# Attention and sixteen experts on one core: the last two units' means rows move to ScalarE's DMA queue, and the last steps of the hand-written order are moved

## The chip, the cores and the metric

The kernel runs on one core of a Trainium2 chip. The metric is the device time of one execution in microseconds (us), the median over the runs. The engines are TensorE (PE), VectorE (DVE), ScalarE (ACT), GpSimd (POOL) and SyncE (SP), which only issues DMAs and loads values.

## The reference

Attention over 8 batches, 8 heads, 576 positions and 64 dimensions per head, in two parts that are added; then a mixture of 16 experts over the 4608 tokens of 512 dimensions:

```python
q_d, k_d, v_d = means of four neighbouring positions      # 144 of each
out_d = softmax(q_d k_d^T / 8) v_d, repeated four times
mask = |i - j| < 4
out_local = softmax(q k^T / 8 where mask) v
x = out_d repeated + out_local                            # 4608 x 512
g = argmax(x @ w_group);  e = argmax(x @ w_expert[g])     # 4 groups of 4
out[token] = p_group * p_expert * (relu(x @ w1[g, e]) @ w2[g, e])
```

## The kernel before

The attention is cut into 16 units; unit u is a pair of batches times a pair of heads, four units to a pair of batches. For every unit the local part is computed as scores in a band, and out_local and the repeated out_d come out of one matmul: the values of the windows (tile vw, `windows(u)`) have rows for the window's positions and, between them, rows for the means' attention (`load_down`). So a unit goes through these steps, each a method of `Attention`:

- `load_k`, `load_q`, `load_v`, `load_windows`: loads, all on SyncE's queue.
- `pool_q`, `pool_k`, `pool_v`: sums over four positions (tiles qd, kd, vd), for late units on GpSimd (L215 to L217), except pool_q of 15.
- `s_down` (L314): scores of the means from kd and qd; `s_down_max`, `s_down_exp` (ScalarE, L348, tile Pd), `soft_down` (L354 on GpSimd, tile sg, then two instructions on VectorE).
- `turn_pd`, `turn_pd_out`, `out_down` (L401), `out_down_out`, `turn_down` (L412), `turn_down_out` (VectorE, tile odn).
- `down_store` (L429, L430): the means' attention goes to DRAM (odd) over SyncE's queue. `load_down` (L434): it comes back into the rows of the windows tile (vw<-odd), over the queue that the order names: S is SyncE's, A is ScalarE's.
- `turn_e`, `turn_e_out`: the band's probabilities, turned (tile pt). `x_bank` (L441, three banks of matmuls b_x<-vw,pt), `x_bank_out` into the tile x (L165 on ScalarE, L167 on VectorE), `store_x` (L451) to the table xd in DRAM, `turn_x`, `logits` (L486, L489).

Tiles that are kept from unit to unit are chosen by `of`: x has three tiles, x_124 in a pool that stays and x_125, x_126 in the pool inp, which is closed by the step `change` and whose room the first expert's tiles take over. Units below 14 take them in turn, units 14 and 15 take the first, so unit 12 is in x_124, unit 13 in x_125, and units 14 and 15 both in x_124.

After each pair of batches the router (`Router`) chooses an expert per token, and its steps `weight` (a small store xd<-cw, L661), `places`, `places_out`, `count`, `lists` (tile m, L671), `lists_places`, `lists_add` and `lists_out` build the experts' token lists. From the first three pairs `pick_early` takes one expert; `early_list` builds its list of 256 tokens of units 0 to 11 (gi), `early_expert` (L1361) reads its number on SyncE, `change` opens the expert's pools, and `gather` (L851) fetches the tokens (xg) by an indirect DMA of GpSimd. Its weights come in four quarters: `weights_in` c (two DMAs raww on SyncE, L831) and `weights_split` c into a high and a low part (ScalarE L838, then GpSimd or VectorE L839). `turn_in` (L867) turns the tokens, `hidden` f (L880) is the first matmul of eighth f, `project` f (L926) the second. When the last pair's lists are there, `gather_late` fetches the expert's remaining tokens, `ranks` sorts the experts by load (VectorE, L787 to L1100; tile roh at L789), and `turn_late` turns the remaining tokens. Then `main` runs the other experts, one after the other, on TensorE.

What sets the order: everything up to `project 7` is issued in the order of the string `ORDER` (L1213 to L1324) inside a manual schedule. An entry is a step, its unit, and sometimes the engine or queue. Each engine works through its instructions in that order and waits at each for what it needs.

Of the kernel before, what the change touches and what calls it, by code (L numbers as in the profile page):

```python
# [54 lines left out]
class Attention:  # L55
# [1254 lines left out]
load_windows 15; s_local_exp 15 1; turn_x_out 13 2 A; out_down 15; lists_places 2; turn_x 13 0; soft_down 15 P; turn_x 13 1; lists 2 P  # L1310
out_down_out 15 A; turn_down 15; turn_x_out 13 1 A; turn_down_out 15; turn_x_out 13 0 A; load_down 14 S; down_store 15 S; early_expert
lists_add 2; turn_e 14 2; logits 13; turn_e 14 1; early_list 1; turn_e_out 14 2 A; change; gather; turn_e 14 0; lists_out 2
turn_e_out 14 1 A; turn_e_out 14 0 A; x_bank 14 2; x_bank 14 0; x_bank 14 1; x_bank_out 14 0 A; x_bank_out 14 1 A; turn_x 14 0
soft_local_sum 15 D; soft_local 15; x_bank_out 14 2 D; turn_e 15 0; store_x 14 A; turn_e_out 15 0 D; turn_x_out 14 0 D; turn_x 14 2
turn_x 14 1; turn_x_out 14 1 D; turn_x_out 14 2 A; weights_in 0; turn_e 15 1; turn_in 0; turn_e_out 15 1 D; weights_split 0 w1 P
load_down 15 S; logits 14; turn_in 1; weights_split 0 w2 P; weights_in 1; turn_e 15 2; turn_e_out 15 2 D; x_bank 15 0; turn_in 2
x_bank_out 15 0 A; x_bank 15 1; x_bank_out 15 1 A; x_bank 15 2; x_bank_out 15 2 D; turn_in 3; weights_in 2; turn_x 15 1; turn_x 15 2
turn_x_out 15 2 D; store_x 15 S; turn_x 15 0; weights_split 1 w1 P; turn_x_out 15 1 D; turn_x_out 15 0 A; hidden 0; weights_split 1 w2 P
weights_in 3; logits 15; scores_out 3; hidden 1; scores_turn 3; project 0; scores_turn_out 3; choose 3; choose_exp 3; choose_first 3
weight 3; hidden 2; project 1; places 3; places_out 3; project 2; weights_split 2 w1 P; lists_places 3; lists 3 P; count 3  # L1320
weights_split 2 w2 P; hidden 3; hidden 4; hidden 5; lists_add 3; early_list 0; gather_late; project 3; ranks; weights_split 3 w1 P
# [107 lines left out]
```

## Time and profile before

| | |
|---|---|
| median of 3 runs | 754.81 us |
| the runs | 747.65, 755.3, 754.81 us |
| the profiled execution | 745.63 us |
| its span in the profile | 743.7 us |
| TensorE busy in the span | 696.0 us (94%) |
| VectorE, ScalarE, GpSimd busy | 461.6, 388.5, 252.9 us |
| mean granted TensorE clock | 0.981 of full |

The profiled execution is one execution by itself; the rows below are from it. Times in the rows are microseconds from the start of the span. A row of a timeline has its start, its duration, the engine, the line, the tiles written and read, how many instructions it joins (x3), and in brackets how long the engine had been idle before it and what released it. A row with "SPq" or "ACTq" is the issue of a DMA, not its transfer.

### The profile page before, as it was taken

Reading aid. Unit: us, or ns where it says so; the run is one execution under the profiler, and the core shown is the slowest. Engines: PE = TensorE matmul, PEld = TensorE weight load, DVE = VectorE, ACT = ScalarE, POOL = GpSimd, SP = SyncE. Lnnn points to the kernel's source line nnn. Section 1 sums busy time; section 2 is a strip of 40 time slices with the busy share of each in tenths; the row PEclk is TensorE's granted clock in tenths of the full one; section 3 lists DMA queues with packets and bytes.
Section 4 is the critical chain, followed back from the end, with each engine's and each line's share of the span. In section 5 each row is a group of like instructions: output and inputs, shape, how many; then the busy total and the mean of one; then the engine's idle time right before and its main releaser. Section 6 shows DMA issues by size and latency. Waiting matters only on the chain. (4 is left out here: it accounts for less than half of the span.)

```text
span 743.7 us, 17951 instructions
## 1 busy us (share of the span) xinstructions
PE 696.0 (94%) x7134; PEld 627.0 (84%) x7135; DVE 461.6 (62%) x821; ACT 388.5 (52%) x830; POOL 252.9 (34%) x301
## 2 busy tenths in 40 slices
PE   7788987898987988999999999999999999999997
PEld 4566765676665867998999999999999999999996
DVE  6777877888885766654545454464655565565641
ACT  6766746666674425643434444454554554555531
POOL 7956654576533633003211221302213213212211
PEclk9889999999999999999999999999999999999999
DMA  9979898889879456845455555646555665665600
GB/s 295 258 182 253 253 279 253 201 221 255 220 189 264 121 163 185 274 152 185 150 169 171 163 171 174 206 142 218 172 186 186 206 201 191 221 191 198 222 31 26
DMA packets 109912, 144.94 MB, mean 195 GB/s; under 512 B 22737, under 2 KB 78545, under 8 KB 109825
## 3 DMA queue, kind: packets, MB, share of 16 engines
q1 hardware_dynamic: 85216, 113.25, 51.9%
q0 software_dynamic: 7088, 21.66, 8.5%
q10 hardware_dynamic: 17520, 8.85, 4.7%
q8 instruction: 57, 0.93, 0.5%
q14 instruction: 31, 0.25, 0.1%
HBM read 122.43 MB, written 22.29 MB: 195 GB/s over the span
## 5 line engine op out<-in xcount | busy, mean ns | idle before, releaser
L880 PE MATMUL ph<-xh,w1h 128*128 128x256 f32 (+13 forms) x512 | 161.1, 316 | 0.0
L851 POOL DMA_INDIRECT xg<-xd,gi x47 | 49.1, 1044 | 324.3 <-ACT yo L954 289.9
L880 PE MATMUL ph<-xl,w1h 128*128 128x256 f32 (+13 forms) x512 | 156.0, 306 | 0.0
L880 PE MATMUL ph<-xh,w1l 128*128 128x256 f32 (+13 forms) x512 | 156.0, 307 | 0.0
L839 DVE TENSOR_TENSOR w2l<-raww,w2h 128x1024 fp32r<-128x1024 f32 x61 | 74.6, 1224 | 75.2 <-ACT w2h L838 61.6
L928 PE MATMUL y<-hl,w2h 128*128 128x416 f32 (+11 forms) x384 | 115.3, 311 | 0.0
L928 PE MATMUL y<-hh,w2l 128*128 128x416 f32 (+11 forms) x384 | 114.3, 308 | 0.0
L838 ACT ACTIVATE w2h<-raww 128x1024 fp32r<-128x1024 f32 x64 | 67.5, 1057 | 74.3 <-PE y L928 56.0
L880 PEld LDWEIGHTS ph<-xh,w1h 128*128 128x128 f32 x512 | 96.2, 188 | 1.4 <-issue 0.2
L880 PEld LDWEIGHTS ph<-xl,w1h 128*128 128x128 f32 x512 | 96.3, 188 | 0.9
L839 DVE TENSOR_TENSOR w1l<-raww,w1h 128x1024 fp32r<-128x1024 f32 x60 | 73.4, 1224 | 37.6 <-ACT w1h L838 31.6
L880 PEld LDWEIGHTS ph<-xh,w1l 128*128 128x128 f32 x512 | 96.1, 188 | 0.3
L885 DVE SCALAR_TENSOR_TENSOR hl<-ph,hh 128x256 fp32r<-128x256 f32 (+13 forms) x128 | 60.3, 477 | 54.8 <-ACT hh L884 52.2
L884 ACT ACTIVATE hh<-ph 128x256 fp32r<-128x256 f32 (+13 forms) x128 | 53.9, 422 | 71.6 <-PE ph L880 66.3
L928 PE MATMUL y<-hh,w2h 128*128 128x416 f32 (+11 forms) x384 | 87.7, 312 | 0.0
L838 ACT ACTIVATE w1h<-raww 128x1024 fp32r<-128x1024 f32 x64 | 67.5, 1056 | 30.5 <-PE ph L880 24.2
L928 PEld LDWEIGHTS y<-hh,w2l 128*128 128x128 f32 x384 | 72.3, 188 | 0.1
L928 PEld LDWEIGHTS y<-hl,w2h 128*128 128x128 f32 x384 | 72.2, 188 | 0.1
L955 POOL DMA_INDIRECT out_dram<-yo,oi x47 | 47.8, 1017 | 66.5 <-ACT yo L954 53.0
L928 PEld LDWEIGHTS y<-hh,w2h 128*128 128x128 f32 x384 | 62.9, 188 | 0.1
L860 ACT ACTIVATE xh<-xt 128x256 fp32r<-128x256 f32 (+14 forms) x68 | 27.0, 420 | 38.3 <-PE xt L867 35.7
L441 PE MATMUL b_x<-vw,pt 126*32 126x128 f32 x1152 | 40.4, 284 | 4.0 <-DMA vw<-odd 2.0
(227 smaller groups left out, 1286.6 us busy)
## 6 DMA issues: line engine op xcount, KB each, us to landing
raww<-in_moe_w_dram SPq DMA_DIRECT2D x128, 512.0 KB
vw<-in_vw_dram SPq DMA_DIRECT2D x32, 378.0 KB
kt<-in_k_dram SPq DMA_DIRECT2D x16, 576.0 KB
qT<-in_q_dram SPq DMA_DIRECT2D x16, 576.0 KB
xd<-x ACTq DMA_DIRECT2D x15, 576.0 KB
vs<-in_vm_dram SPq DMA_DIRECT2D x16, 448.0 KB
vw<-odd SPq DMA_DIRECT2D x16, 144.0 KB
vs<-in_vm_dram SPq DMA_DIRECT2D x16, 128.0 KB
```

Source lines behind the costliest of these rows:

```text
L441: self.nc.tensor.matmul(pt[32 * j : 32 * j + 32, t], self.of("pt", u)[:ROWS, 32 * lin : 32 * lin + 32], self.windows(u)[:ROWS, :, lin], st ...
L838: self.nc.scalar.activation(hi, raw, AF.Copy)
L839: eng.tensor_tensor(out=lo, in0=raw, in1=hi.bitcast(F32), op=ALU.subtract)
L851: self.nc.gpsimd.indirect_dma_start(out=xg[:w], out_offset=None, in_=self.xd[0:rows], in_offset=bass.IndirectOffsetOnAxis(ap=st["gi"][:w, ...
L860: self.nc.scalar.activation(hi, x, AF.Copy)
L880: nc.tensor.matmul(ph, a[:, k, cs], st[b][:, k], start=(n == 0), stop=(n == 11))
L884: nc.scalar.activation(hh, ph, AF.Relu)
L885: nc.vector.scalar_tensor_tensor(out=hl, in0=ph, scalar=0.0, in1=hh.bitcast(F32), op0=ALU.max, op1=ALU.subtract)
L928: nc.tensor.matmul(y, a[:, f % 2, cs], b, start=(f == 0 and n == 0), stop=(f == 7 and n == 2))
L955: i = nc.gpsimd.indirect_dma_start(out=self.out, out_offset=bass.IndirectOffsetOnAxis(ap=oi, axis=0), in_=yo[:m], in_offset=None, bounds_c ...
```

## The change

Three things are changed, and nothing in the steps themselves.

- `of` gives the tile x differently for units 12 to 15: unit 12 goes to x_125, units 13 and 14 to x_124, and unit 15 to the first 1152 columns of the windows tile of unit 14 (vw_100), which x_bank 14 has read by then.
- `load_down` of units 14 and 15 stands on ScalarE's queue: the first behind out_down_out 15, the second between two copies of x_bank 14.
- The last 22 lines of `ORDER` are written anew (21 now). On SyncE load_v 15, load_windows 14 and weight 2 stand ahead of load_down 13. On GpSimd soft_down 14 stands ahead of pool_k 15. Of the third pair's router places_out, count, lists_places, lists, pick_early, lists_add and lists_out stand further up, and with them early_list and gather. turn_pd_out 15 2 goes from VectorE to ScalarE. Of the early expert's weights the splits of quarters 2 and 3 stand further up and w2 of quarter 3 goes from VectorE to GpSimd; hidden 6 stands ahead of the four steps turn_late, which were two and two around it.

```diff
@@ class Attention
     def of(self, n, u):
 
         t = self.kept[n]
+        if n == "x" and u > 11:
+            return (t[1], t[0], t[0], self.vw[0][:, 0, 0 : 2 * G].rearrange("p (g a) d -> p g (a d)", a=2))[u - 12]
         return t[u % len(t) if u < LATE_UNITS else 0]
...
@@ ORDER
-turn_pd 14 0; turn_pd 14 2; turn_x_out 12 1 A; turn_pd_out 14 0 A; turn_pd_out 14 2 A; pool_k 15 P; pick_early; turn_pd 14 1; s_down 15
-load_v 15; turn_pd_out 14 1 A; turn_x 12 2; store_x 12 A; turn_x_out 12 2 A; load_windows 14; soft_down 14 P; out_down 14; x_bank 13 1
+soft_down 14 P; soft_local_sum 14 D; turn_x_out 12 0 A; turn_pd 14 0; turn_pd 14 2; turn_x_out 12 1 A; turn_pd_out 14 0 A
+turn_pd_out 14 2 A; pool_k 15 P; turn_pd 14 1; s_down 15; turn_pd_out 14 1 A; turn_x 12 2; store_x 12 A; turn_x_out 12 2 A; out_down 14
...
-project 4; project 5; turn_late 0; turn_late 1; hidden 6; turn_late 2; turn_late 3; hidden 7; weights_split 3 w2 D; project 6; rank_lists
-project 7
+project 4; project 5; hidden 6; turn_late 0; turn_late 1; turn_late 2; turn_late 3; hidden 7; project 6; rank_lists; project 7
```

Behind `of` the kernel after is two lines longer, so L434 is L436 there and so on.

GpSimd around pool_k 15 (kd_3594 from kt_91), before; sg_118 is soft_down 14, vd_112 is pool_v 15, m the third pair's lists:

```order
L217 TENSOR_TENSOR vd_111<-vd_111,vs_115 112x384
L215 TENSOR_TENSOR kd_3594<-kt_91 128x288
L216 TENSOR_TENSOR kd_3594<-kd_3594,kt_91 128x288
L217 TENSOR_TENSOR kd_3594<-kd_3594,kt_91 128x288
L354 TENSOR_SCALAR sg_118<-sg_118 128x5
L215 TENSOR_TENSOR vd_112<-vs_113 112x384
L216 TENSOR_TENSOR vd_112<-vd_112,vs_113 112x384
L217 TENSOR_TENSOR vd_112<-vd_112,vs_113 112x384
L354 TENSOR_SCALAR sg_119<-sg_119 128x5
L671 TENSOR_TENSOR m_3792<-oh,chl 128x9x64
```

The same place after, where pool_k 15 is kd_3626:

```order
L219 TENSOR_TENSOR vd_111<-vd_111,vs_115 112x384
L356 TENSOR_SCALAR sg_118<-sg_118 128x5
L217 TENSOR_TENSOR kd_3626<-kt_91 128x288
L218 TENSOR_TENSOR kd_3626<-kd_3626,kt_91 128x288
L219 TENSOR_TENSOR kd_3626<-kd_3626,kt_91 128x288
L217 TENSOR_TENSOR vd_112<-vs_113 112x384
L218 TENSOR_TENSOR vd_112<-vd_112,vs_113 112x384
L219 TENSOR_TENSOR vd_112<-vd_112,vs_113 112x384
L673 TENSOR_TENSOR m_3732<-oh,chl 128x9x64
L356 TENSOR_SCALAR sg_119<-sg_119 128x5
```

pool_k 15 stood ahead of soft_down 14 and now stands behind it; lists 2 has moved ahead of soft_down 15 (sg_119).

SyncE from load_windows 15 (vw_101) on, before; vw_100 is the windows tile of unit 14, odd the means' attention in DRAM, raww the early expert's weights:

```order
L200 DMA vw_101<-in_vw_dram 42x2x1152 x2
L434 DMA vw_100<-odd_89 8x72x64
L429 DMA odd_90<-odn_131 128x2x128
L430 DMA odd_90<-odn_131 32x128
L1361 TENSOR_LOAD eri_168
L1361 ISA x2
L831 ISA
L831 DMA raww_3944<-in_moe_w_dram 128x4x256
L831 ISA
L831 DMA raww_3946<-in_moe_w_dram 128x2x512
L434 DMA vw_101<-odd_90 8x72x64
L831 ISA
```

And after:

```order
L202 DMA vw_101<-in_vw_dram 42x2x1152 x2
L431 DMA odd_90<-odn_131 128x2x128
L432 DMA odd_90<-odn_131 32x128
L1362 TENSOR_LOAD eri_168
L1362 ISA x2
L833 ISA
L833 DMA raww_3945<-in_moe_w_dram 128x4x256
L833 ISA
L833 DMA raww_3947<-in_moe_w_dram 128x2x512
L833 ISA
L833 DMA raww_3980<-in_moe_w_dram 128x4x256
L833 ISA
```

Both load_down are gone from SyncE; the second pair of weights now follows the first directly.

ScalarE around the copies of x_bank 14 (x_124 from b_x_14), before:

```order
L165 ACTIVATE xT<-b_xt_13_3781 128x384
L165 ACTIVATE pt_122<-b_e_14_3827 126x384
L687 ACTIVATE tab<-tab_3816 128x128
L165 ACTIVATE pt_122<-b_e_14_3835 126x384
L165 ACTIVATE pt_122<-b_e_14_3870 126x384
L165 ACTIVATE x_124<-b_x_14_3890 128x384
L165 ACTIVATE x_124<-b_x_14_3903 128x384
L451 DMA xd<-x_124 128x9x128
L165 ACTIVATE xT<-b_xt_14_3934 128x3x128
```

And after:

```order
L167 ACTIVATE od_129<-b_od_3790 128x288
L436 DMA vw_100<-odd_89 8x72x64
L167 ACTIVATE xT<-b_xt_13_3803 128x384
L167 ACTIVATE xT<-b_xt_13_3799 128x384
L167 ACTIVATE pt_122<-b_e_14_3858 126x384
L167 ACTIVATE pt_122<-b_e_14_3866 126x384
L167 ACTIVATE pt_122<-b_e_14_3871 126x384
L167 ACTIVATE x_124<-b_x_14_3890 128x384
L436 DMA vw_101<-odd_90 8x72x64
L167 ACTIVATE x_124<-b_x_14_3903 128x384
L453 DMA xd<-x_124 128x9x128
L167 ACTIVATE xT<-b_xt_14_3935 128x3x128
```

load_down 14 (vw_100<-odd_89) stands behind out_down_out 15 (od_129), load_down 15 (vw_101<-odd_90) between the two copies of x_bank 14, one row and a copy ahead of store_x 14.

## Rows read from the trace of the kernel before

**Rows 1.** busy us by window, PE PEld DVE ACT POOL; granted clock; DMA share; GB/s

```profile
230.00:240.00 10.00, 7.29 (x118) 4.98 (x115) 3.85 (x9) 4.56 (x9) 3.44 (x2) 1.00 0.88 257
...
260.00:270.00 10.00, 6.61 (x39) 4.99 (x38) 8.56 (x19) 2.50 (x7) 3.17 (x2) 1.00 0.41 132
...
280.00:290.00 10.00, 8.06 (x37) 6.17 (x36) 4.71 (x8) 3.92 (x9) 2.60 (x2) 0.83 0.69 206
...
400.00:500.00 100.00, 100.00 (x676) 99.59 (x675) 52.58 (x73) 48.11 (x77) 18.15 (x18) 1.00 0.53 170
```

**Rows 2.** TensorE's timeline, 213 to 242 us: start, duration, line, tiles, [idle before <-releaser]

```profile
213.01 1.15 PE L314 MATMUL b_d<-kd,qd 64*128 64x144 f32 x20
...
228.12 1.94 PE L441 MATMUL b_x<-vw,pt 126*32 126x128 f32 x60 [2.03 <-DMA vw<-odd]
...
236.25 0.86 PE L441 MATMUL b_x<-vw,pt 126*32 126x128 f32 x24
...
240.29 0.44 PE L867 MATMUL xt<-idf,xg 128*128 128x128 f32 x2 [1.35 <-ACT x L165]
...
241.66 0.39 PE L880 MATMUL ph<-xh,w1h 128*128 128x256 f32 x1
```

**Rows 3.** ScalarE's timeline, 231 to 240 us (ACTq: its DMA issues)

```profile
231.49 0.37 ACTq L451 DMA_DIRECT2D xd<-x  x1
...
239.74 0.87 ACT L165 ACTIVATE x<-b_x 128x384 f32<-128x384 f32 x2 [1.77 <-DMA xd<-x]
```

**Rows 4.** GpSimd's timeline, 200 to 230 us

```profile
204.50 0.94 POOL L217 TENSOR_TENSOR kd<-kd,kt 128x288 f32<-128x288 f32 x1
211.80 0.20 POOL L354 TENSOR_SCALAR sg<-sg 128x5 f32<-128x5 f32 x1 [6.36 <-ACT Pd L348]
...
227.28 1.29 POOL L851 DMA_INDIRECT xg<-xd,gi  x1 [5.92 <-DMA odd<-odn]
```

**Rows 5.** SyncE's DMA issues, 226 to 242 us

```profile
226.28 0.98 SPq L831 DMA_DIRECT2D raww<-in_moe_w_dram  x2
228.44 0.77 SPq L434 DMA_DIRECT2D vw<-odd  x1
229.43 9.92 SPq L831 DMA_DIRECT2D raww<-in_moe_w_dram  x3
```

**Rows 6.** DMA by queue (packets, MB, share), 228 to 231 us: q1 SyncE's, q0 GpSimd's

```profile
q1 hardware_dynamic: 715, 0.96, 91.2%
```

**Rows 7.** DMA by queue, 231 to 233.5 us

```profile
q0 software_dynamic: 114, 0.35, 51.9%
q1 hardware_dynamic: 734, 0.33, 50.3%
```

**Rows 8.** DMA by queue, 233.5 to 236 us: q10 is ScalarE's

```profile
q1 hardware_dynamic: 552, 0.71, 95.0%
...
q10 hardware_dynamic: 2, 0.00, 0.1%
```

**Rows 9.** DMA by queue, 236 to 239 us

```profile
q10 hardware_dynamic: 1161, 0.59, 75.6%
```

**Rows 10.** TensorE's timeline, 262 to 270 us

```profile
263.17 0.44 PE L867 MATMUL xt<-idf,xg 128*128 128x128 f32 x2 [1.35 <-DMA xg<-xd,gi]
...
268.54 0.50 PE L926 MATMUL y<-w2h,hh 128*128 128x512 f32 x1 [1.48 <-ACT w2h L838]
...
269.80 0.50 PE L926 MATMUL y<-w2l,hh 128*128 128x512 f32 x1 [0.53 <-DVE w2l L839]
```

**Rows 11.** VectorE's timeline, 260 to 264 us

```profile
260.71 2.77 DVE L789 TENSOR_TENSOR roh<-rank,eidx 128x256 f32<-128x256 f32 x1
```

**Rows 12.** TensorE's timeline, 284 to 290 us

```profile
284.34 0.44 PE L904 MATMUL ht<-idf,hr 128*128 128x128 f32 x2 [1.15 <-ACT hr L899]
...
286.17 0.63 PE L926 MATMUL y<-w2h,hrl 128*128 128x512 f32 x1
...
289.22 0.39 PE L926 MATMUL y<-w2h,hrl 128*128 128x512 f32 x1
```

More of the change, by code (lines that the diff above doesn't have):

```diff
@@ L1302 @@
 x_bank 12 1; s_down 14; down_store 13 S; pool_q 15 D; load_windows 13; s_local_exp 15 0; lists_out 1; x_bank_out 12 1 A; choose_first 2
-x_bank 12 0; choose_exp 2; x_bank 12 2; s_down_max 14; x_bank_out 12 0 A; places 2; turn_x 12 0; load_down 13 S; turn_x 12 1
-soft_local_sum 14 D; x_bank_out 12 2 A; s_down_exp 14 0; pool_v 14; s_down_exp 14 2; s_down_exp 14 1; count 2; turn_x_out 12 0 A
-turn_pd 14 0; turn_pd 14 2; turn_x_out 12 1 A; turn_pd_out 14 0 A; turn_pd_out 14 2 A; pool_k 15 P; pick_early; turn_pd 14 1; s_down 15
@@ L1306 @@
-load_v 15; turn_pd_out 14 1 A; turn_x 12 2; store_x 12 A; turn_x_out 12 2 A; load_windows 14; soft_down 14 P; out_down 14; x_bank 13 1
-s_down_max 15; weight 2; s_down_exp 15 2; out_down_out 14 A; turn_down 14; x_bank 13 2; s_down_exp 15 0; s_down_exp 15 1; x_bank_out 13 1 A
-pool_v 15; x_bank 13 0; turn_pd 15 0; x_bank_out 13 2 A; turn_down_out 14; soft_local 14; x_bank_out 13 0 A; turn_pd_out 15 0 A
-places_out 2; store_x 13 A; turn_pd 15 1; down_store 14 S; turn_x 13 2; turn_pd 15 2; turn_pd_out 15 1 A; logits 12; turn_pd_out 15 2 D
@@ L1310 @@
[L1310 to L1321, printed above, removed]
@@ L1322 @@
-project 4; project 5; turn_late 0; turn_late 1; hidden 6; turn_late 2; turn_late 3; hidden 7; weights_split 3 w2 D; project 6; rank_lists
-project 7
+x_bank 12 0; choose_exp 2; x_bank 12 2; s_down_max 14; x_bank_out 12 0 A; places 2; load_v 15; load_windows 14; weight 2; turn_x 12 0
+load_down 13 S; turn_x 12 1; places_out 2; count 2; x_bank_out 12 2 A; s_down_exp 14 0; pool_v 14; s_down_exp 14 2; s_down_exp 14 1
+soft_down 14 P; soft_local_sum 14 D; turn_x_out 12 0 A; turn_pd 14 0; turn_pd 14 2; turn_x_out 12 1 A; turn_pd_out 14 0 A
@@ new lines @@
+turn_pd_out 14 2 A; pool_k 15 P; turn_pd 14 1; s_down 15; turn_pd_out 14 1 A; turn_x 12 2; store_x 12 A; turn_x_out 12 2 A; out_down 14
+x_bank 13 1; s_down_max 15; s_down_exp 15 2; out_down_out 14 A; turn_down 14; x_bank 13 2; s_down_exp 15 0; s_down_exp 15 1
+x_bank_out 13 1 A; pool_v 15; x_bank 13 0; turn_pd 15 0; x_bank_out 13 2 A; lists_places 2; turn_down_out 14; lists 2 P; soft_local 14
+pick_early; soft_down 15 P; x_bank_out 13 0 A; turn_pd_out 15 0 A; store_x 13 A; turn_pd 15 1; down_store 14 S; turn_x 13 2; turn_pd 15 2
@@ new lines @@
+turn_pd_out 15 1 A; turn_pd_out 15 2 A; logits 12; lists_add 2; load_windows 15; s_local_exp 15 1; turn_x_out 13 2 A; lists_out 2
+out_down 15; turn_x 13 0; turn_x 13 1; out_down_out 15 A; load_down 14 A; early_list 1; turn_down 15; turn_x_out 13 1 A; turn_down_out 15
+turn_x_out 13 0 A; down_store 15 S; early_expert; change; gather; turn_e 14 2; logits 13; turn_e 14 1; turn_e_out 14 2 A; turn_e 14 0
+turn_e_out 14 1 A; turn_e_out 14 0 A; x_bank 14 2; x_bank 14 0; x_bank 14 1; x_bank_out 14 0 A; load_down 15 A; x_bank_out 14 1 A
@@ new lines @@
+turn_x 14 0; soft_local_sum 15 D; soft_local 15; x_bank_out 14 2 D; turn_e 15 0; store_x 14 A; turn_e_out 15 0 D; turn_x_out 14 0 D
+turn_x 14 2; turn_x 14 1; turn_x_out 14 1 D; turn_x_out 14 2 A; weights_in 0; turn_e 15 1; turn_e 15 2; turn_in 0; turn_e_out 15 1 D
+weights_split 0 w1 P; logits 14; turn_in 1; weights_split 0 w2 P; weights_in 1; turn_e_out 15 2 D; x_bank 15 0; turn_in 2; x_bank_out 15 0 A
+x_bank 15 1; x_bank_out 15 1 A; x_bank 15 2; x_bank_out 15 2 D; turn_in 3; weights_in 2; turn_x 15 1; turn_x 15 2; turn_x_out 15 2 D
@@ new lines @@
+store_x 15 S; turn_x 15 0; weights_split 1 w1 P; turn_x_out 15 1 D; turn_x_out 15 0 A; hidden 0; weights_split 1 w2 P; weights_in 3
+logits 15; scores_out 3; hidden 1; scores_turn 3; project 0; scores_turn_out 3; weights_split 2 w1 P; choose 3; choose_exp 3
+weights_split 2 w2 P; choose_first 3; weight 3; hidden 2; project 1; places 3; places_out 3; project 2; lists_places 3; lists 3 P; count 3
+weights_split 3 w1 P; hidden 3; hidden 4; hidden 5; lists_add 3; early_list 0; gather_late; project 3; ranks; weights_split 3 w2 P
```

## The prediction

> **What bounds the kernel now.** I read the busy time by window first [rows 1]. From 400 to 500 us TensorE is busy for 100.00 of 100 us: the sixteen experts follow each other without a gap, so nothing the change does can shorten that part. What it can move is the moment at which TensorE becomes gapless. Before that moment stand 230 to 240 us with 7.29 us busy of 10, 260 to 270 us with 6.61, and 280 to 290 us with 8.06 at a granted clock of 0.83. Every microsecond by which TensorE's work up to about 290 us shifts goes straight into the end time, and nothing else does.
>
> Then I read TensorE's own timeline there for the waits [rows 2]. s_down of unit 15 starts at 213.01 with no wait. x_bank of unit 14 starts at 228.12, after 2.03 us of waiting for its means rows (vw<-odd, load_down 14). x_bank of unit 15 starts at 236.25 with none. At 240.29 TensorE has lost 1.35 us to ScalarE's copy of x, and that copy itself waited 1.77 us, until 239.74, for the store of unit 14 (xd<-x) to leave the tile that unit 15 writes next [rows 3]. That store was issued at 231.49. The first expert's first matmul (hidden 0) is at 241.66. These are the places the change touches.
>
> Durations are from the profiled execution: 743.7 us of span and 745.63 us in all. The median of the runs shown is 754.81, 9.18 us above it; I make the sum against the profiled execution and carry the shift over to the median unchanged.
>
> **Part 1: soft_down 14 ahead of pool_k 15 on GpSimd (a new wait).** Before, the three sums of pool_k 15 (kd) end with the one at 204.50, which takes 0.94 us, so three take about 2.8 us; the small sg instruction of unit 14 comes behind them at 211.80, when ScalarE's Pd is there [rows 4]. Now kd stands behind sg: 211.80 + 0.20 + 2.8 is 214.8. s_down 15 needs kd, so it goes from 213.01 to about 215: 2.0 us later, with the issue between them. Queued behind it on TensorE is everything: out_down 14, x_bank 13, out_down 15, and through these the means rows of units 14 and 15. The cover is the 2.03 us wait before x_bank 14: if load_down 14 lands as before, the 2.0 us vanish there. But load_down 14 is itself a product of the delayed work, so I bound x_bank 14's shift by 0 and 2.0 and take 1.4, nearer to the second because its source is late too. pool_v 15 and the POOL steps behind it move likewise by under 3 us; out_down 15 is also later by 2, which covers most of that.
>
> **Part 2: load_down 13 behind other SP transfers.** It is issued some microseconds later than before, behind load_v 15, load_windows 14 and weight 2's store; x_bank 13 is itself late by 2.0 us and comes far enough behind it. I cost it at nothing; if it landed late, each microsecond would add to the 2.0 of part 1.
>
> **Part 3: load_down 14 and 15 on ScalarE's queue.** On SP, load_down 15 stood between the two pairs of early weights: the first pair (raww) was issued at 226.28, load_down 15 at 228.44, the next weights from 229.43 [rows 5]. Now SP has nothing between the pairs and issues four weight transfers in a row, while load_down 15 stands on ScalarE behind a copy of x_bank 14. Its place there is just ahead of store_x 14, issued at 231.49 before [rows 3], so with the shift of 1.4 at about 232. SP's weights follow the store of unit 15's means, which moves by about 2, so they go from about 228.3; two issues took 0.98 us, four are done by about 230.3. So load_down 15 is issued behind four weight transfers instead of two, and I must know whether another engine's queue gets past them.
>
> The transfers by queue say no. From 228 to 231 us queue q1 (SP's) moved 0.96 MB, the first pair; from 231 to 233.5 it moved 0.33 MB, load_down 15's small packets, beside the gather's 0.35 MB on q0; from 233.5 to 236 it moved 0.71 MB, while q10 (ScalarE's), on which store_x 14 had stood since 231.49, moved 2 packets; only from 236 to 239 did q10 move 1161 packets [rows 6 to 9]. Hardware transfers were served in the order of their issue, whichever engine issued them. The Trainium skill (DMA: Bandwidth & Descriptors, Queues, rings and completion order) states instead that each DMA engine alternates between the queues it has work for, a packet at a time; by that rule load_down 15 would slip past the weights, and the time would be that of the first rival below. The trace does not agree for these two queues.
>
> So the second pair, 1 MB, goes ahead of load_down 15. Before, all four weights and load_down 15 were through when q10 began to move, at about 236; that stretch now begins about 2 us later (with SP's weights), so load_down 15 is through at about 238 and, with about 1 us from its last packets to the waiting matmul, x_bank 15 starts at 239. Bounds: 237.3, where TensorE's own work gets there if the load is no limit (236.25 plus about 1), and 241, if the gather's packets fall beside it once more. I take 239, as it comes from the nearest rows.
>
> **Part 4: x of unit 15 in its own tile.** The 1.77 us wait of ScalarE for store_x 14 goes, and with it TensorE's 1.35. From x_bank 15 to hidden 0 it took 241.66 - 236.25 = 5.41 us; without the 1.35, and with x's last copy just in time, 4.1 to 4.7. From 239 that puts hidden 0 at 243.7 at most and 243.1 at least; middle 243.4, about 1.8 us later than before. What is late next in place of the store wait is load_down 15 itself: a wait of roughly 3 us before x_bank 15 that wasn't there.
>
> **Part 5: gather and early list earlier.** The gather was issued at 227.28 after 5.92 us of waiting [rows 4]. Its list still hangs on TensorE and VectorE steps that part 1 delays, so it gains 0 to 1.5 us; I take 1. TensorE meets it (xt) ahead of x_bank 15, where it waits for load_down 15 anyway: worth nothing on the path.
>
> **Part 6: hidden 6 ahead of turn_late; the last splits earlier, w2 of quarter 3 on GpSimd.** Between 262 and 270 us TensorE waited 1.35 us for the late gather, 1.48 for ScalarE's w2h and 0.53 for VectorE's w2l [rows 10], 3.36 together. Now hidden 6 covers the first, and the split stands early enough for the other two. But VectorE is held by one instruction of 2.77 us (roh) from 260.71 [rows 11], and the four turn_late steps, now in one piece, need VectorE to free their banks behind it. So the gain is between 0 and 3.36; I take 1.6, the middle.
>
> **Sum.** +1.8 at hidden 0, -1.6 in 262 to 270, nothing elsewhere: +0.2. 745.63 + 0.2 = 745.8 for the profiled execution, 754.81 + 0.2 = 755.0 for the median. From its parts: hidden 0 from 0 to +3.8 and a gain of 0 to 3.36 give -3.4 to +3.8, so 751.4 to 758.6.
>
> **The rivals.** *The transfers aren't in order (faster).* If load_down 15 gets past the weights, it lands before TensorE needs it: x_bank 15 at about 237.3 at the latest, no store wait. Then hidden 0 gains the 1.35, less what part 1 left: with the gather 1 us earlier TensorE reaches x_bank 15 at 236, so hidden 0 is at about 240.3, 1.4 earlier, and with 1.6 from part 6 the sum is -3.0: 751.8. For it: q0's gather did move beside q1 [rows 7]. Against it: q10 with its 2 packets [rows 8].
>
> *The disturbance at 280 to 290 goes (faster).* TensorE lost 1.15 us to ScalarE's hr at 284.34, and then a matmul 512 wide took 0.63 us instead of 0.39 [rows 12], one of six, at a granted clock of 0.83 for the ten microseconds, a mean between the chip's 1.2 and 2.4 GHz [rows 1], the only such dip of these windows. Busy time lacks 1.94 us, and six times 0.24, at most 1.4 since they overlap, make about 1.1 more: 3.0. The late tokens' order around it changes a little, so it may not come back: +0.2 - 3.0 = -2.8, 752.0.
>
> *load_down 15 served beside the gather (slower).* Place: the DMA queues from 230 to 240. Beside the gather q1 moved 0.33 MB in 2.5 us, 0.13 MB/us, against 0.32 MB/us without it [rows 6, 7]. If the second pair of weights, about 1 MB, is what meets the gather, it takes 7.7 us instead of 3.1; x_bank 15 and all behind it then come 4.6 us later: +0.2 + 4.6 = +4.8, 759.6. It decides from the point where x_bank 15 starts after 241, for then part 6 no longer pays it back. For it: the gather moves up towards the weights. Against it: large packets suffer less than the small ones of load_down 15, on which that slow rate was measured.
>
> *Nothing moves.* TensorE is the bound and its work is the same; if parts 1 and 3 are covered and 6 is spent, the time is 754.8.
>
> **How the numbers follow.** Forecast (with "nothing moves", which it can't be told from) 0.53, out-of-order transfers 0.2, dip gone 0.12, gather beside 0.15. A measurement of this kernel tells about 1%, 7.5 us, from no change. None of the cases alone goes that far, so most chance is within 1%. Both faster cases together make -6.0, and the runs of before themselves reach from 747.65 to 755.3; a median that falls among the low ones would read as faster: 0.13. The slow case with its price a little short, or one more lost wait of 2 us, passes the bound: 0.10. Range: from 746, both faster cases and the low end of the runs, to 760, the slow case.
>
> **What would show it.** Right: s_down 15 at about 215 released by POOL; q1's four weights before load_down 15, and x_bank 15 waiting 2 to 5 us for vw<-odd and starting near 239; ScalarE's copy of x 15 without a wait for xd<-x; hidden 0 near 243.4; less idle time in 262 to 270. Wrong: x_bank 15 without a wait (then the queues are not served in order, and I am too slow), s_down 15 still at 213, or hidden 0 past 246.

## The result: 1.08% slower

The changed kernel has a median of 757.78 us against 751.95 for the kernel before, measured together; the ratio is 1.0108, 95% interval 1.0084 to 1.0131. (The ratio compares undisturbed runs alone, so it isn't the quotient of the two medians, 1.0078.) The profiled execution took 758.05 us, its span is 756.0 (before: 745.63 and 743.7).

The windows of the changed kernel, to be held against [rows 1] (columns: length, busy time and instruction count of PE, PEld, DVE, ACT and POOL, granted clock, DMA share, GB/s):

```profile
210.00:220.00 10.00, 6.27 (x55) 4.68 (x57) 7.37 (x29) 5.37 (x21) 5.92 (x8) 0.78 0.72 184
220.00:230.00 10.00, 10.00 (x133) 7.20 (x131) 6.09 (x18) 6.41 (x24) 1.18 (x2) 0.71 0.23 47
...
240.00:250.00 10.00, 4.39 (x66) 2.82 (x67) 2.26 (x6) 3.31 (x6) 4.65 (x2) 0.66 0.95 277
...
260.00:270.00 10.00, 7.46 (x35) 6.01 (x34) 9.21 (x21) 0.82 (x1) 6.53 (x4) 0.67 0.13 30
...
400.00:500.00 100.00, 100.00 (x665) 99.55 (x664) 51.37 (x72) 46.37 (x74) 18.13 (x18) 1.00 0.54 175
```

From 400 us on nothing has changed. The loss lies between 210 and 270 us, and in four of these windows TensorE is granted less than the full clock (0.78, 0.71, 0.66, 0.67, means between its two levels), and in three of the four it waits besides (busy 6.27, 4.39 and 7.46 of 10 us). Before, [rows 1] has 1.00 in 230 to 240 and 260 to 270.

TensorE's timeline shows where (to be held against [rows 2] and [rows 10]):

```profile
216.82 1.97 PE L316 MATMUL b_d<-kd,qd 64*128 64x144 f32 x20 [1.92 <-POOL kd L219]
...
221.88 1.51 PE L443 MATMUL b_x<-vw,pt 126*32 126x128 f32 x24
...
235.47 2.17 PE L443 MATMUL b_x<-vw,pt 126*32 126x128 f32 x72 [1.13 <-DMA vw<-odd]
...
246.83 1.51 PE L443 MATMUL b_x<-vw,pt 126*32 126x128 f32 x24 [5.61 <-DMA vw<-odd]
...
252.14 0.37 PE L882 MATMUL ph<-xh,w1h 128*128 128x256 f32 x1
...
263.23 0.22 PE L612 MATMUL pos<-oh,tri 128*128 128x144 bf16 x1 [2.13 <-DVE oh L599]
...
265.58 0.63 PE L928 MATMUL y<-w2l,hh 128*128 128x512 f32 x1
...
281.58 0.33 PE L869 MATMUL xt<-idf,xg 128*128 128x128 f32 x1 [1.96 <-DVE hl L887]
```

s_down 15 waits 1.92 us for kd, and it and what follows run slowly (1.97 us instead of 1.15; 24 matmuls of x_bank 13 take 1.51 instead of 0.86). x_bank 15 waits 5.61 us for its means rows. Then comes a wait that I had not forecast at all: 2.13 us for VectorE's oh (the tokens' chosen experts, which the router's matmul reads), and behind it a stretch in which a 512-wide matmul takes 0.63 us instead of 0.39. The last row is a wait of 1.96 us for hl, the low part of the expert's hidden values, which VectorE computes.

GpSimd (against [rows 4]), then the DMA issues of SyncE and of ScalarE (against [rows 5] and [rows 3]):

```profile
213.69 0.20 POOL L356 TENSOR_SCALAR sg<-sg 128x5 f32<-128x5 f32 x1 [9.15 <-ACT Pd L350]
...
215.84 0.93 POOL L219 TENSOR_TENSOR kd<-kd,kt 128x288 f32<-128x288 f32 x1
...
231.96 1.29 POOL L853 DMA_INDIRECT xg<-xd,gi  x1 [7.81 <-PE b_e L364]
```

```profile
232.10 0.36 SPq L431 DMA_DIRECT2D odd<-odn  x1
...
234.19 12.64 SPq L833 DMA_DIRECT2D raww<-in_moe_w_dram  x6
```

```profile
237.11 0.66 ACTq L436 DMA_DIRECT2D vw<-odd  x1
...
249.27 0.48 ACT L167 ACTIVATE vw<-b_x 128x384 f32<-128x384 f32 x1
```

kd ends at 216.77, straight behind sg, as part 1 had it. SyncE issues four weight transfers in a row from 234.19 to 236.96 (the other two of the row's six come at 244.16), load_down 15 follows on ScalarE at 237.11, and TensorE can use it at 246.83, 9.7 us later. The copy of x 15 has no wait for a store any more.

DMA by queue in the changed kernel, first 238 to 242 us, then 242 to 244, against [rows 6 to 9] (the share adds up the packets' own times, so it can pass 100%):

```profile
q1 hardware_dynamic: 1066, 1.40, 105.0%
...
q10 hardware_dynamic: 31, 0.01, 0.9%
```

```profile
q1 hardware_dynamic: 177, 0.32, 53.3%
q10 hardware_dynamic: 689, 0.24, 46.2%
```

With load_down 15 standing on q10 since 237.11, q10 moves 31 packets until 242 while q1 moves 1.40 MB of weights: order of issue again, in the main. It is not strict, for from 242 to 244 both queues move.

What holds VectorE up is seen when its rows are laid beside GpSimd's; VectorE of the changed kernel, then GpSimd:

```profile
258.76 2.05 DVE L597 TENSOR_TENSOR o<-t,m2x 128x180 f32<-128x180 f32 x1
260.85 2.33 DVE L599 TENSOR_TENSOR oh<-o 128x144 bf16<-128x144 f32 x1
```

```profile
258.00 2.60 POOL L841 TENSOR_TENSOR w1l<-raww,w1h 128x1024 fp32r<-128x1024 f32 x1 [0.37 <-ACT w1h L840]
260.57 2.44 POOL L841 TENSOR_TENSOR w2l<-raww,w2h 128x1024 fp32r<-128x1024 f32 x1
```

Before, the same two VectorE instructions took 0.35 and 0.31:

```profile
248.29 0.35 DVE L595 TENSOR_TENSOR o<-t,m2x 128x180 f32<-128x180 f32 x1
248.67 0.31 DVE L597 TENSOR_TENSOR oh<-o 128x144 bf16<-128x144 f32 x1
```

Each ends 0.2 us behind the GpSimd split that was running when it began (260.81 against 260.60, 263.18 against 263.01). These are the splits of quarter 2, which the change moved among choose 3, choose_exp 3 and choose_first 3.

### The profile page after: what moved, and what is told of

Same layout as the page of the kernel before. It is cut to its first block, busy times and chain, and to the rows that moved or that the text cites. A ratio compares the mean times of both kernels' runs of the same rounds, so it can differ in the third digit from the quotient of the medians.

```text
span 756.0 us, 17950 instructions
## 1 busy us (share of the span) xinstructions
PE 702.0 (93%) x7134; PEld 632.0 (84%) x7135; DVE 462.2 (61%) x819; ACT 388.7 (51%) x831; POOL 255.8 (34%) x302
## 5 line engine op out<-in xcount | busy, mean ns | idle before, releaser
L840 ACT ACTIVATE w1h<-raww 128x1024 fp32r<-128x1024 f32 x64 | 67.5, 1057 | 29.9 <-PE ph L882 24.1
L443 PE MATMUL b_x<-vw,pt 126*32 126x128 f32 x1152 | 43.7, 300 | 15.0 <-DMA vw<-odd 9.1
L443 PEld LDWEIGHTS b_x<-vw,pt 126*32 126x32 f32 x1152 | 34.7, 121 | 21.8 <-issue 14.1
```

Source lines behind the costliest of these rows:

```text
L443: self.nc.tensor.matmul(pt[32 * j : 32 * j + 32, t], self.of("pt", u)[:ROWS, 32 * lin : 32 * lin + 32], self.windows(u)[:ROWS, :, lin], st ...
L840: self.nc.scalar.activation(hi, raw, AF.Copy)
```

## The experiments

There are three theories, one for each loss. **C**: the moved GpSimd splits hold VectorE, so that TensorE waits for oh. **P**: pool_k 15 behind soft_down 14 delays all that follows. **L**: load_down 15 is served behind four weight transfers. Each run has its ratio to the kernel before of the same runs. To see where a run's time went I read four starts from TensorE's timeline of its profiled execution: s_down 14, hidden 0, the first matmul of the gapless part (the first 416 wide), and the span's end.

| run | ratio, 95% interval | starts and end | s_down 14 to hidden 0 | to gapless | to end |
|---|---|---|---|---|---|
| before | 1 | 204.49, 241.66, 290.37, 743.7 | 37.2 | 48.7 | 453.3 |
| changed | 1.0108 (1.0084 to 1.0131) | 206.24, 252.14, 302.10, 756.0 | 45.9 | 50.0 | 453.9 |
| undo_split2 | 1.0067 (1.0031 to 1.0104) | 207.64, 254.12, 302.00, 755.5 | 46.5 | 47.9 | 453.5 |
| undo_pool | 1.0022 (0.9977 to 1.0068) | 203.12, 244.30, 293.02, 746.3 | 41.2 | 48.7 | 453.3 |
| undo_ld15 | 1.0042 (1.0007 to 1.0077) | 205.76, 246.71, 298.85, 752.1 | 41.0 | 52.1 | 453.3 |
| undo_three | 0.9985 (0.9946 to 1.0024) | 207.56, 245.44, 293.13, 746.4 | 37.9 | 47.7 | 453.3 |
| alone_split2 | 1.0081 (1.0038 to 1.0125) | 205.21, 247.53, 297.67, 751.0 | 42.3 | 50.1 | 453.3 |
| alone_pool | 1.0032 (1.0000 to 1.0065) | 204.77, 247.27, 291.89, 745.2 | 42.5 | 44.6 | 453.3 |
| alone_x15_hidden6 | 1.0008 (0.9975 to 1.0040) | 205.38, 240.94, 290.98, 744.3 | 35.6 | 50.0 | 453.3 |
| changed_weights_later | 1.0066 (1.0040 to 1.0093) | 207.09, 245.68, 296.63, 749.9 | 38.6 | 51.0 | 453.3 |
| undo_four | 0.9975 (0.9936 to 1.0015) | 204.19, 239.15, 286.29, 739.7 | 35.0 | 47.1 | 453.4 |
| alone_load_downs | 0.9957 (0.9912 to 1.0001) | 203.73, 246.47, 292.57, 745.9 | 42.7 | 46.1 | 453.3 |
| pair_pool_loads | 1.0088 (1.0049 to 1.0127) | 205.41, 250.16, 294.75, 748.1 | 44.8 | 44.6 | 453.4 |
| splits_on_vector | 0.9956 (0.9913 to 0.9999) | 206.19, 241.62, 287.33, 741.0 | 35.4 | 45.7 | 453.7 |

The last column is the same in all within 0.6 us: that the gapless part passes every shift on to the end, on which the whole prediction stood, holds. The middle columns are of one execution each; the ratio is the measurement. How much one execution scatters is seen in runs whose code is the same up to hidden 0: 37.2 and 42.3 (before, alone_split2), 45.9 and 46.5 (changed, undo_split2), 37.9 and 35.0 (undo_three, undo_four), 35.6 and 35.4 (alone_x15_hidden6, splits_on_vector). A difference of a few us between two of these columns shows nothing by itself.

**undo_split2**

```diff
-... scores_turn_out 3; weights_split 2 w1 P; choose 3; choose_exp 3
-weights_split 2 w2 P; choose_first 3; weight 3; hidden 2; ...
-project 2; lists_places 3; ...
+... scores_turn_out 3; choose 3; choose_exp 3; choose_first 3; weight 3; hidden 2; ...
+project 2; weights_split 2 w1 P; lists_places 3; lists 3 P; count 3
+weights_split 2 w2 P; weights_split 3 w1 P; hidden 3; ...
```

> The changed kernel with only the splits of quarter 2 put back behind project 2 and count 3. Theory C (two GpSimd splits that run beside VectorE's choose 3 stretch its instructions from 0.3 to over 2 us, TensorE then waits 2.13 us for oh and loses speed): VectorE's o and oh take under 0.5 us again, TensorE has no wait for oh, no slow stretch from 263 to 270; the gapless part starts about 5 us sooner, ratio to before about 1.004. Rival L (all the loss comes from load_down 15 and pool_k 15 before hidden 0): the wait for oh goes but returns at the late lists, ratio stays at 1.009 or more.

Measured 1.0067. VectorE's two instructions are short again and the wait for oh is gone:

```profile
260.73 0.34 DVE L597 TENSOR_TENSOR o<-t,m2x 128x180 f32<-128x180 f32 x1
261.11 0.31 DVE L599 TENSOR_TENSOR oh<-o 128x144 bf16<-128x144 f32 x1
```

The mechanism of theory C holds; of the 5 us expected some 2 show in the profile (50.0 to 47.9), 0.4% in the ratio. The rival is right in part: TensorE now waits 1.87 us for the late gather instead.

**undo_pool**

```diff
-soft_down 14 P; soft_local_sum 14 D; ...
-turn_pd_out 14 2 A; pool_k 15 P; turn_pd 14 1; s_down 15; ...
+soft_local_sum 14 D; ...
+turn_pd_out 14 2 A; pool_k 15 P; soft_down 14 P; turn_pd 14 1; s_down 15; ...
```

> The changed kernel with only pool_k 15 ahead of soft_down 14 on GpSimd again. Theory P (the 1.92 us wait of s_down 15 and the slow stretch behind it are pool_k's place): s_down 15 has no wait for kd, the matmuls from 214 to 226 run at full speed, x_bank 14 starts 3 to 5 us sooner after s_down of unit 14 than in the changed kernel; ratio about 1.005. Rival: x_bank 14 and load_down 15 hang on DMAs that do not move, hidden 0 gains under 1 us, ratio 1.009 or more.

Measured 1.0022, more than theory P wanted. s_down 15 has no wait, x_bank 14 comes 24.0 us after s_down 14 (227.13 - 203.12) instead of 29.2 (235.47 - 206.24). x_bank 15 still stands idle for 4.82 us (the profile names no releaser there), so this is P's loss and not L's.

**undo_ld15**

```diff
-x_bank_out 14 0 A; load_down 15 A; x_bank_out 14 1 A
+x_bank_out 14 0 A; x_bank_out 14 1 A
-weights_split 0 w1 P; logits 14;
+weights_split 0 w1 P; load_down 15 S; logits 14;
```

> The changed kernel with only load_down 15 back on SyncE's queue between the two pairs of early weights. Theory L: x_bank 15's wait for vw<-odd falls from 5.61 us to under 2, hidden 0 comes about 4 us sooner, ratio about 1.005. Rival (the wait comes from late data of unit 15, not from the weights ahead of it): the wait stays over 4 us and the ratio at 1.009 or more.

Measured 1.0042, about as theory L has it. The wait falls from 5.61 us to 2.25 (under 2 was expected), and hidden 0 comes 4.9 us sooner (41.0 against 45.9):

```profile
241.15 1.22 PE L443 MATMUL b_x<-vw,pt 126*32 126x128 f32 x24 [2.25 <-DMA vw<-odd]
```

**undo_three** (the three edits above together)

> The changed kernel with all three put back (splits of quarter 2, pool_k 15, load_down 15). If the three are the whole loss and add up, the time is that of before less the store wait of x 15 (1.35 us) and 1 to 2 us at the late tokens: ratio 0.996 to 1.000. If something else in the change costs, it stays above 1.003.

Measured 0.9985: the loss is gone. The three account for the whole of it. Singly they make 0.41, 0.86 and 0.66%, in sum 1.93, together 1.23; each of these differences has an interval of 0.4 to 0.5 to both sides, so whether they add up is not shown here.

**alone_split2**

```diff
-scores_turn_out 3; choose 3; choose_exp 3; choose_first 3
+scores_turn_out 3; weights_split 2 w1 P; choose 3; choose_exp 3; weights_split 2 w2 P; choose_first 3
```

with the two splits taken out of the lines below, in the kernel before.

> The kernel before with one part of the change alone: the two splits of quarter 2 beside choose 3, on GpSimd. Theory C: VectorE's o and oh take over 2 us each while GpSimd splits, TensorE waits about 2 us for oh; from hidden 0 to the late tokens' first matmul it takes 33 us or more instead of 30.57; ratio 1.003 to 1.005. Rival (harmless without the other parts): ratio within 0.998 to 1.002.

Measured 1.0081, beyond what theory C wanted. VectorE and GpSimd:

```profile
254.17 2.05 DVE L595 TENSOR_TENSOR o<-t,m2x 128x180 f32<-128x180 f32 x1
256.25 2.33 DVE L597 TENSOR_TENSOR oh<-o 128x144 bf16<-128x144 f32 x1
```

```profile
253.41 2.60 POOL L839 TENSOR_TENSOR w1l<-raww,w1h 128x1024 fp32r<-128x1024 f32 x1 [0.37 <-ACT w1h L838]
255.98 2.44 POOL L839 TENSOR_TENSOR w2l<-raww,w2h 128x1024 fp32r<-128x1024 f32 x1
```

The same 2.05 and 2.33 us as in the changed kernel, a wait of TensorE for oh of 2.12 us, and then a granted clock of 0.71 from 260 to 270. To the late tokens' first matmul (L896) it takes 35.8 us from hidden 0 (283.30 - 247.53), where the kernel before takes 30.6. From hidden 0 to the gapless part it takes 50.1 us, against 44.6, 46.1 and 44.6 in alone_pool, alone_load_downs and pair_pool_loads, whose code from hidden 0 on is that of before: 4 to 5.5 us, 0.5 to 0.7%. (Its 42.3 us up to hidden 0 are not the edit's, which comes later; in that execution TensorE stood idle for 2.25 and 3.24 us at the gather's turns, in the kernel before for 0.94.)

**alone_pool**

```diff
-turn_pd_out 14 2 A; pool_k 15 P; pick_early;
+turn_pd_out 14 2 A; soft_down 14 P; pool_k 15 P; pick_early;
```

> The kernel before with one part alone: soft_down 14 ahead of pool_k 15 on GpSimd. Theory P: s_down 15 waits about 1.9 us for kd and the matmuls behind it run slow for a stretch; from s_down 14 to hidden 0 it takes 40 us or more instead of 37.17; ratio 1.003 to 1.007. Rival (the cover I counted on: the 2.03 us wait ahead of x_bank 14 swallows it): 37 to 38 us, ratio within 0.998 to 1.002.

Measured 1.0032 (1.0000 to 1.0065), at the lower end of theory P's range and at the edge of no change. s_down 15 waits 1.24 us and takes 1.97. The 42.5 us to hidden 0 prove little beside alone_split2's 42.3 with the old code there, but x_bank 14 comes 28.5 us after s_down 14 (233.30 - 204.77), in alone_split2 24.1 (229.32 - 205.21). The cover of 2.03 us that I counted on did not swallow the delay: x_bank 14 waits 2.23 us as well.

**alone_x15_hidden6**

```diff
-        return t[u % len(t) if u < LATE_UNITS else 0]
+        if n == "x" and u > 11: ...   # as in the change
-turn_late 0; turn_late 1; hidden 6; turn_late 2; turn_late 3;
+hidden 6; turn_late 0; turn_late 1; turn_late 2; turn_late 3;
```

> The kernel before with the two parts that I counted as gains and nothing else: x of unit 15 in its own tile, and hidden 6 ahead of the four turn_late steps. If they are worth what I said, TensorE's waits for x of 15 (1.35 us) and for the late gather (1.35 us) go and the ratio is 0.995 to 0.997. Rival (each wait comes back as the next one, at the logits or at VectorE's sorting): ratio 0.999 to 1.001.

Measured 1.0008: the rival. The store wait is gone, and hidden 0 comes 1.6 us sooner in this execution (35.6 against 37.2), less than such columns scatter. But another VectorE instruction, cw, now begins 0.05 us after a GpSimd split instead of before it, takes 2.34 us instead of 0.18, and TensorE waits 1.72 us for hl. VectorE, GpSimd and TensorE:

```profile
249.76 2.34 DVE L662 TENSOR_TENSOR cw<-two 128x9 f32<-128x9 f32 x1
```

```profile
249.71 2.35 POOL L841 TENSOR_TENSOR w1l<-raww,w1h 128x1024 fp32r<-128x1024 f32 x1 [3.02 <-ACT w1h L840]
```

```profile
252.48 0.80 PE L928 MATMUL y<-w2h,hl 128*128 128x512 f32 x1 [1.72 <-DVE hl L887]
```

So what the store wait gives, a hold of VectorE can take back; splits_on_vector, the last run below, puts that to the test.

**changed_weights_later** (in the changed kernel; load_down 15 stays on ScalarE's queue)

```diff
-turn_e 15 0; store_x 14 A; turn_e_out 15 0 D;
+turn_e 15 0; turn_e_out 15 0 D;
-weights_split 0 w2 P; weights_in 1;
+weights_split 0 w2 P; store_x 14 S; weights_in 1;
```

> The changed kernel with load_down 15 left on ScalarE's queue, but store_x 14 put on SyncE ahead of the second pair of early weights, so that this pair is issued after load_down 15. Theory L (transfers are served in the order of issue, whichever queue): x_bank 15's wait for vw<-odd falls from 5.61 us to under 3 and hidden 0 comes about 3 us sooner, as with load_down 15 on SyncE; ratio about 1.005. Rival (ScalarE's queue is itself the slow one): the wait stays over 4.5 us and the ratio at 1.009.

ScalarE's DMA issue, then SyncE's, then TensorE:

```profile
237.05 0.66 ACTq L436 DMA_DIRECT2D vw<-odd  x1
```

```profile
239.16 1.77 SPq L833 DMA_DIRECT2D raww<-in_moe_w_dram  x2
```

```profile
241.63 0.86 PE L443 MATMUL b_x<-vw,pt 126*32 126x128 f32 x24
```

The same transfer on the same queue at the same time (237.05, changed kernel 237.11) serves TensorE at most 4.6 us later instead of 9.7, without a wait, once the second pair of weights is issued behind it. It is the order of issue, not ScalarE's queue. Hidden 0 comes 7.3 us sooner (38.6 against 45.9). The ratio of 1.0066 is short of that; from hidden 0 on it takes 51.0 us, with the wait for oh still there (1.07 us) and one of 2.85 us for hl.

**undo_four** (undo_three, and quarter 3's splits back)

```diff
-weights_split 3 w1 P; hidden 3; ...; ranks; weights_split 3 w2 P
+hidden 3; ...; ranks; weights_split 3 w1 P
-hidden 7; project 6;
+hidden 7; weights_split 3 w2 D; project 6;
```

> The changed kernel with four parts put back: pool_k 15, load_down 15, and the places and engines of all splits of quarters 2 and 3; what stays is x of 15 in its own tile, load_down 14 on ScalarE, the earlier lists and hidden 6. Theory C in full (quarter 3's splits on GpSimd cost too, as hidden 0 to the last expert's start took 47.69 us in the run with three parts back against 44.62 with the old tail): hidden 0 to the gapless part 45 us or less; ratio 0.993 to 0.997. Rival (quarter 3 is harmless): 47 to 48 us, ratio 0.998 to 1.000.

Measured 0.9975, between the two expected ranges, and 47.1 us from hidden 0, as the rival has it. Quarter 3's splits can't be told from harmless.

**alone_load_downs**

```diff
-load_down 14 S; down_store 15 S;
+down_store 15 S;                     # load_down 14 A behind out_down_out 15 A
-load_down 15 S; logits 14;
+logits 14;                           # load_down 15 A behind x_bank_out 14 0 A
```

> The kernel before with one part alone: load_down 14 and 15 on ScalarE's queue. Theory L: x_bank 15 waits for vw<-odd behind the four weight transfers, 2 to 5 us, less the store wait of 1.35 us that it hides; hidden 0 comes 39 to 41 us after s_down 14 instead of 37.17; ratio 1.002 to 1.005. Rival (the queue is free and its issue earlier): 37 us or less, ratio 0.998 to 1.000.

Measured 0.9957, interval to 1.0001: theory L's loss doesn't show when the rest is as before. The 42.7 us to hidden 0 fit neither expectation. In this execution x_bank 15 has no wait for vw<-odd; TensorE waited before it, 2.72 us at the gather's first turn and then 1.74 for its data:

```profile
236.40 0.30 PE L867 MATMUL xt<-idf,xg 128*128 128x128 f32 x1 [2.72 <-issue]
238.44 0.47 PE L867 MATMUL xt<-idf,xg 128*128 128x128 f32 x1 [1.74 <-DMA xg<-xd,gi]
...
241.11 1.51 PE L441 MATMUL b_x<-vw,pt 126*32 126x128 f32 x24
```

In this execution load_down 15's delay stands behind the gather's, and by the ratio the part costs nothing that can be measured.

**pair_pool_loads** (alone_pool and alone_load_downs together)

> The kernel before with two parts together: soft_down 14 ahead of pool_k 15, and load_down 14 and 15 on ScalarE's queue. If the two feed each other (the later s_down 15 delays load_down 15's issue further behind the weights), hidden 0 comes 43 us or more after s_down 14, x_bank 15 waits over 3 us for vw<-odd, and the ratio is 1.006 or more, above the sum of the two alone. Rival (they add up, 1.0032 and 0.9957): ratio 0.997 to 1.002.

Measured 1.0088, against 1.0032 and 0.9957 alone: they feed each other, though not by the wait I named, for x_bank 15 again has none for vw<-odd; TensorE loses 3.1 and 2.5 us at the gather's turns in front of it, but 2.7 and 1.7 us in alone_load_downs too, so by what they feed each other is not shown. Hidden 0 comes 44.8 us after s_down 14, close to the changed kernel's 45.9.

**splits_on_vector** (alone_x15_hidden6, and two splits off GpSimd)

```diff
-weight 3; hidden 2; project 1; places 3; places_out 3; project 2; weights_split 2 w1 P; ...
+weight 3; hidden 2; weights_split 2 w1 D; project 1; places 3; places_out 3; project 2; ...
-project 3; ranks; weights_split 3 w1 P
+project 3; weights_split 3 w1 D; ranks
```

> The kernel before with the two gains (x of 15 in its own tile, hidden 6 ahead of turn_late) and two splits taken off GpSimd: w1 of quarter 2 behind hidden 2 and w1 of quarter 3 ahead of the sorting, both on VectorE. Theory C: VectorE's cw and roh take under 0.7 us again instead of 2.34 and 2.79, TensorE's waits for hl go, hidden 0 to the gapless part takes 44 us or less, ratio 0.992 to 0.996, faster than both kernels. Rival (VectorE becomes the bound of these steps, as it now does 1.2 us more per split): ratio 0.999 to 1.003.

Measured 0.9956 (0.9913 to 0.9999), 742.54 us against 749.02: the interval just excludes no change against the kernel before, and it lies well below the changed kernel's. TensorE's waits for hl are gone. From hidden 0 to the gapless part it takes 45.7 us, not the 44 expected, against 50.0 in alone_x15_hidden6. A split costs VectorE 1.22 us, but the sorting's roh, 2.77 us in [rows 11], takes 0.43, and cw 0.18 instead of the 2.34 of alone_x15_hidden6:

```profile
250.44 0.18 DVE L662 TENSOR_TENSOR cw<-two 128x9 f32<-128x9 f32 x1
250.86 1.22 DVE L841 TENSOR_TENSOR w1l<-raww,w1h 128x1024 fp32r<-128x1024 f32 x1
...
261.85 0.43 DVE L791 TENSOR_TENSOR roh<-rank,eidx 128x256 f32<-128x256 f32 x1
```

## Why the prediction was wrong, point by point

The measured 757.78 us lies inside the range, but the forecast was no change (755.0, within 1%), and the kernel became 1.08% slower, to which I had given 0.10. The sum was +0.2 us; the span grew by 12.3 in the profiled executions and the median by 5.8. Both terms of the sum failed: hidden 0 came 8.7 us later than before, counted from s_down 14 (45.9 against 37.2), not 1.8, and the stretch behind it lost time instead of gaining 1.6.

One thing lies under the whole sum: the profiled execution that I read was not a typical one. Its mean granted clock was 0.981. In the 114 executions of the kernel before that were timed beside the experiments (one of 2287.93 us left out) the mean granted clock is 0.970 on average and 0.981 at most. So the clock stood at 1.00 in three of the four windows of [rows 1], while the kernel before usually runs with less, and a shift from that one execution to the median is not the change's alone.

**The late tokens' term, part 6, has the wrong sign**: "the split stands early enough for the other two", and hidden 6 "covers the first", together counted as a gain of 1.6 us in 262 to 270. I priced the moved splits by what TensorE no longer waits for, and took the GpSimd time as free. In the changed kernel the three waits of 3.36 us are gone, but waits of 2.13 us for oh and of 0.42 and 1.96 us for hl have come, 4.51 together. To the late tokens' first matmul (L896, L898 after) it takes 34.0 us from hidden 0 (286.18 - 252.14) instead of 30.6 (272.23 - 241.66), and alone the split's edit costs 0.81%, some 6 us. The wait of 1.96 us stands where hidden 6 was to cover the gather: in eight of the nine executions with hidden 6 in front TensorE waits 1.30 to 2.19 us for hl there, which VectorE makes behind roh; in splits_on_vector, where roh is short, it doesn't.

The clue stood in my own rows: roh of 2.77 us [rows 11] was read as a long instruction, while it was a short one (0.43 us in splits_on_vector) held by the GpSimd split beside it, which ended at 263.19 against roh's 263.48. GpSimd, before:

```profile
260.81 2.38 POOL L839 TENSOR_TENSOR w1l<-raww,w1h 128x1024 fp32r<-128x1024 f32 x1
```

The Trainium skill (SBUF — State Buffer, Who interferes with whom) says that a VectorE instruction with two SBUF inputs contends with a GpSimd instruction that reads SBUF, and that the one which issues first has the shared ports for its whole length. The traces agree with the first half in all places shown: 0.35 to 2.05, 0.31 to 2.33, 0.18 to 2.34 and 0.43 to 2.77 us. So does the kernel before: beside the split of 250.43 a reduction, with one input, took its usual 0.30 us, and the next instruction, with two, took 1.01 us (0.21 in the changed kernel) and ended 0.06 us behind the split:

```profile
250.43 2.40 POOL L839 TENSOR_TENSOR w1l<-raww,w1h 128x1024 fp32r<-128x1024 f32 x1 [3.26 <-ACT w1h L838]
```

```profile
251.54 0.30 DVE L625 TENSOR_REDUCE pos<-sl 128x9 f32<-128x144 f32 x1
251.88 1.01 DVE L626 TENSOR_TENSOR ge<-pos,steps 128x45 f32<-128x45 f32 x1
```

The second half the rows don't show for roh: its row starts 0.10 us before the split's (260.71 and 260.81), as it does in all 13 executions where a split runs beside it, and it is held in each (2.76 to 2.82 us).

**Part 1 had the wait right and its price wrong.** Forecast 2.0 us for kd, measured 1.92. But I took 1.4 us as the shift at x_bank 14, and it is 5.6, seen from s_down 14 (29.2 against 23.6). What I did not price is TensorE's clock behind the wait: from s_down 15's start to the end of x_bank 13, in which TensorE has no wait in either trace, it takes 9.6 us (216.82 to 226.43) instead of 5.8 (213.01 to 218.79). In all six profiled executions with the kd wait (changed, undo_split2, undo_ld15, alone_pool, changed_weights_later, pair_pool_loads) x_bank 14 comes 27.1 to 30.0 us after s_down 14, in the eight without it 23.1 to 25.7. In those six the granted clock in 210 to 230 us fell below 1.00, to 0.57 to 0.78 in the lower of the two windows; of the eight without it, three fell too. alone_load_downs fell to 0.66 with no such wait, so the wait is not the only cause, and what else is stays open.

**Part 3 was right in mechanism and short in size.** Order of issue was shown twice, by the queues and by changed_weights_later. I expected x_bank 15 at 239 after a wait of roughly 3 us; it starts at 246.83 after 5.61. Most of this is when the weights start, not how long they take. They follow the store of unit 15's means, which I had moved by about 2 us; it moved by 8.1 (232.10, shown above, against 224.00 below), and the weights came at 234.19 instead of 228.3. This is part 1's delay again: counted from s_down 14 that store is issued after 19.5 us before, 25.9 in the changed kernel and 20.8 in undo_pool (223.87 - 203.12). From their first issue to x_bank 15 it is 12.6 us where I had 10.7. SyncE, before:

```profile
224.00 0.37 SPq L429 DMA_DIRECT2D odd<-odn  x1
```

The Trainium skill's rule of alternating queues (DMA: Bandwidth & Descriptors, Queues, rings and completion order) would have let load_down 15 in between the weights; q10's 31 packets in 4 us are against it. That the part costs nothing alone (alone_load_downs) and the pair costs 0.88% I had not foreseen: I added up parts that are not independent.

**Part 4 held**: the store wait is gone. What it is worth is not measured: hidden 0 comes 1.6 us sooner in alone_x15_hidden6, within the scatter, and its ratio shows nothing. **Part 5** erred in sign: the gather was issued 25.7 us after s_down 14 (231.96 - 206.24), not earlier than the 22.8 of before (227.28 - 204.49) but later. Part 1 delays it: with pool_k 15 put back (undo_pool) it is issued 20.6 us after s_down 14 (223.72 - 203.12). It cost nothing, as x_bank 15 waited anyway. (Of the steps listed as moved further up, pick_early moved down, from beside pool_k 15 to behind lists 2.) **The rivals**: the slower one had the right sign and place, and x_bank 15 did start after 241, but its agent, the gather, was not what was new. It did run beside the weights (from 234 to 237 us, in part their start, q0 moved 0.45 MB and q1 0.15), but so it had before [rows 7]. That its +4.8 us is near the median's +5.8 is chance. The disturbance at 280 to 290 [rows 12] did go, in the changed kernel and in alone_pool with the old code alike, so it belonged to that one execution, which I had carried into the sum as if it were the kernel.

## What to carry to other kernels

Before moving elementwise work on GpSimd, list the VectorE instructions with two SBUF inputs that will run beside it, and price each at the rest of the GpSimd instruction, as here; a long VectorE row in the old trace may be such a hold and not its own length. Moving a transfer to another engine's queue changed here when it was issued; it still stood behind what had been issued before it. Parts of a change must be priced together, not only one by one: here one cost nothing, the other 0.3%, and both 0.9%. Before a sum is built on one profiled execution, hold its granted clock and time against the other runs of the same kernel.

## What the runs showed of the hardware that I had not expected

Two GpSimd splits in a row hold two VectorE instructions in a row: oh, 0.31 us by itself, began at 260.85, after the next split had begun at 260.57, and was held to 263.18. After TensorE's wait for oh (1.07 to 2.14 us) the granted clock fell in each of the five executions that had it, for instance to 0.67 (changed) and 0.71 (alone_split2) in 260 to 270 us, against 1.00 before; the 512-wide matmuls there took 0.63 us instead of 0.39. Waits as long or longer elsewhere, such as the 2.03 us in [rows 2] and 3.64 us ahead of x_bank 14 in alone_x15_hidden6, left the clock at 1.00, so the length alone doesn't decide it.
